# Window attention, a rational FFN and a gated FFN on one core: block 0's first part divided among three engines by rule, weight words put together in PSUM, later attention tied to phases

## The chip, the core and the metric

The kernel runs on one core of one Trainium2 chip. The metric is the device time of one execution, in microseconds (us). Engines: TensorE (PE; its weight loads are PEld), VectorE (DVE), ScalarE (ACT), GpSimd (POOL), and SyncE (SP), which issues the DMAs.

## What is computed

Three layers follow one another. Attention has 4 x 8 heads of 64 features over 576 positions with a causal window of 64. Then 2304 tokens of 512 features go through an FFN with a rational function, 512 -> 2048 -> 512, and through a gated one, 512 -> 1536 -> 512.

```python
scores = scale * np.matmul(q, k.transpose(0, 1, 3, 2))
mask = (rel >= 0) & (rel < window)
scores = np.where(mask, scores, -1000000000.0)
attn = softmax(scores)
x = np.matmul(attn, v)

h = x @ w_in
P = a[0] + a[1] * h + a[2] * h**2 + a[3] * h**3
Q = 1.0 + np.abs(b[0]) * np.abs(h) + np.abs(b[1]) * h**2
x = (P / (Q + 1e-06)) @ w_out

gate = 1.0 / (1.0 + np.exp(-(x @ w_gate)))
return gate * (x @ w_val) @ w_out2
```

The weights arrive as 64-bit floats and the other inputs as 32-bit ones.

## The kernel before

**Precision.** Each fp32 product of the FFNs is three TensorE passes: an operand is split into a high part (rounded to the fp32r type, `hi`) and a low part (what is left, `lo`), and hi x hi, hi x lo and lo x hi are added in PSUM.

**Tiling.** The 2304 tokens are five blocks of 512, 256, 512, 512 and 512. The work of one block and one FFN is a phase: "part 1" is the rational FFN (`step1`, 16 steps f of 128 hidden features), "part 2" the gated one (`step2`, 12 steps). Phases run: part 1 and 2 of block 0, then part 1 of blocks 1 and 2, part 2 of blocks 1 and 2, and so for 3 and 4. A step of part 1 is 12 matmuls into a PSUM bank h, a chain of elementwise operations, and 12 matmuls into four y banks. A step of part 2 has 12 matmuls each into h (gate) and a (value), a sigmoid, a product, the split, and 12 matmuls into y.

**The chain of a step of part 1** (line of the kernel before in brackets): `size` |h| (730) and `cubic` a3 h (734) on ScalarE; `slope` (739, 743) and `quad` (748), which make Q; two `horner` steps (751) on VectorE, with h from PSUM; `log` (757) and `seed` exp (760) on ScalarE, a first 1/Q; `check` (763) and `newton` (768) refine it, or `check`, `rest` (774, 776) and `correct` (779) do the same in three; `ratio` (782); `hi` (316 ScalarE, 318 VectorE, 320 GpSimd) and `lo` (323).

**Attention.** A unit is 128 tokens and all heads: units 0 to 3 belong to block 0, 4 and 5 to block 1, 6 to 9 to block 2, and so on. In each: scores (546, 557), peak (571), exps (579), inverse (588, 589), norm (593), transposes on TensorE (604) or, from unit 10, on VectorE (621), values (630), and the split into x.

**Weights.** A chunk is 128 x 512. In the first use of each chunk its 64-bit floats are turned into fp32 with integer instructions: DMA into `wraw` (3 tiles), `rescale` (414, 416) of the high word into a temporary `wt`, `sign` (422 VectorE, 427 GpSimd), `shift` (430) and `low_bits` (435) on VectorE, then `hi` and `lo`. Chunks that are used again are stored to DRAM and loaded from there (477). In block 0's first part 32 such chunks (w_in and w_out) are made, in its second part 36.

**What sets the order.** The kernel doesn't write its order by hand. Each operation is registered with a due time (`prio`), the engines that may do it with a cost each (`ways`), what it needs (`deps`), and the tile slots that it takes and uses. `Plan.order` places the operations one after the other: at each moment, by due time, each goes to the engine that would end it first by these costs, if its slots are free; `PORT` marks costs that GpSimd and VectorE may not spend at the same time. The result is one list; each engine works through its part in that order at run time, and waits where an input isn't there. Slots: 28 chunks w, 3 wraw (s), 11 temporaries t, 2 split tiles g; PSUM has 8 banks: 4 y, 2 h, 2 a.

Of the kernel before, what the change touches and what calls it, by code (L numbers as in the profile page):

```python
# [216 lines left out]
def pe(n, count=1):  # L217
    return ("PE", count * (n / 2400 + 0.0025))


def act(n, psum=False, ptrs=0):
    return ("ACT", n / 1200 + (0.05 if psum else 0.093) + 0.093 * ptrs)


def dve(n, ptrs=0):

    return ("DVE", n / 960 + 0.15 + 0.03 * ptrs, *PORT)
# [7 lines left out]
def dve2(n, ptrs=0):  # L235
    return ("DVE", n / 1920 + 0.15 + 0.03 * ptrs, *PORT)
# [6 lines left out]
def pool1(n, ptrs=0):  # L243
    return ("POOL", n / 960 + 0.07 + 0.03 * ptrs, *PORT)
# [7 lines left out]
def tile_window_attention__rational_ffn__glu(  # L252
# [58 lines left out]
    def temp(slot, name, dt=F32):  # L311
        return tile_of(slot, [P, 512], dt, name)
# [83 lines left out]
    def weights(c, prio, keys, again):  # L396

        raw_s, t_s, w_s = Slot("s"), Slot("t"), Slot("w")  # L400
        z = {}
# [6 lines left out]
        def rescale(e):  # L408
            t = z["t"] = temp(t_s, "wt", U32)
            w = z["c"] = tile_of(w_s, [P, 2, 512], F32R, "w")  # L410
            z["hi"], z["lo"] = w[:, 0, :], w[:, 1, :]
            x = z["high"].bitcast(F32)
            if e == "ACT":
                nc.scalar.activation(out=t.bitcast(F32), in_=x, func=AF.Copy, scale=REBIAS * REBIAS)  # L414
            else:
                ENGINES[e].tensor_scalar(
                    out=t.bitcast(F32), in0=x, scalar1=REBIAS, scalar2=REBIAS, op0=ALU.mult, op1=ALU.mult
                )
# [27 lines left out]
        def store(e):  # L446
# [4 lines left out]
        o = before["load"] = op(  # L451
            -200.47 + 0.92 * before.get("n", 0) if before.get("n", 0) < 8 else prio - 6.66,
            [dma(4096 * P)], load, takes=[raw_s], after=before.get("load")
        )
        before["n"] = before.get("n", 0) + 1
        o = before["size"] = before["take"] = op(
            prio, [act(512), dve2(512), pool1(512)], rescale, [o, before.get("size")], [t_s, w_s], [raw_s],
            before.get("take"),
        )
        o = op(prio, [pool1(512), dve2(512)], sign, [o], uses=[raw_s])  # L460
        o = op(prio, [dve(512)], shift, [o], uses=[t_s, raw_s])
        o = op(prio, [dve(512)], low_bits, [o], uses=[t_s, raw_s])
# [25 lines left out]

    def unit(u, t0, prio_load, prio_v):
        first_block = u < UB[0]  # L490
# [175 lines left out]
        for j in range(2):  # L666
            o = sc = op(
                t(j), [pe(512, (5 if first_block else 4) + on_pe)], scores(j), [lk, sc],
                [s_s[j]] + [sm_s][j:], {q_s, k_s},
# [44 lines left out]
    def step1(p, b, fs, f, t0):  # L714
# [97 lines left out]
        G = op(t0 + 1.06, [act(n, True, 1)], cubic, [H, coef], [g_s], [h_s])  # L812
        Q = op(t0 + 2.74, [dve2(n, 2), act(n, False, 2), pool1(n, 2)], slope, [A, coef], [q_s], [a_s])
        Q = op(t0 + 1.97, [pool(n), dve(n)], quad, [Q], uses=[q_s, a_s])
        G = op(t0 + 0.94, [dvep(n, 1)], horner(2), [G], uses=[g_s, h_s])
# [3 lines left out]
        Q = op(t0 + 0.6, [dve(n)], check, [L], uses=[r_s, q_s])  # L819
        if b == 0 and f % 4 < 1:  # L820
            Q = op(t0 + 0.6, [act(n, False, 1), dve2(n), pool1(n)], rest, [Q], uses=[q_s])
            L = op(t0 + 2.52, [pool(n), dve(n)], correct, [Q], uses=[r_s, q_s])
        else:
            L = op(t0 + 2.52, [dve(n)], newton, [Q], uses=[r_s, q_s])
        G = op(t0 + 4.38, [dve(n, 1)], ratio, [L, G], uses=[r_s, g_s])
        X = op(t0 + 4.16, [act(n), dve2(n), pool1(n)], hi, [G], [gs_s], [g_s])
        X = op(t0 + 3.61, [pool(n), dve(n)], lo, [X], uses=[gs_s, g_s])
        for ms in [range(KD)] if f != last_f else [(m,) for m in range(KD)]:
# [30 lines left out]
    def step2(p, b, fs, f, t0):  # L859
# [221 lines left out]
```

## Time and profile before

| | us |
|---|---|
| median of 3 runs | 1024.69 |
| lowest, highest | 1024.28, 1024.74 |
| profiled execution | 1018.68 |
| its span, first to last instruction | 1016.9 |
| PE busy | 960.3 (94%) |
| DVE busy | 725.7 (71%) |
| ACT busy | 484.8 (48%) |
| POOL busy | 200.7 (20%) |

The page divides the span into 40 slices of 25.4 us and gives each engine's busy share in tenths. A "group" is all instructions of one line, engine and operation: busy time, the mean of one, and the idle time just before them with what ended it. An instruction's shown duration overlaps the next one's start by some tens of nanoseconds, so what one costs in a full queue is the distance between two starts; the busy time of a window counts overlapped time once.

### The profile page before, as it was taken

How to read it: one execution, taken by the hardware profiler on the slowest of the kernel's cores; microseconds unless marked ns; L12 is line 12 of the kernel's file. 1: busy time of each engine (PE TensorE's matmuls, PEld its weight loads, DVE VectorE, ACT ScalarE, POOL GpSimd, SP SyncE). 2: the span in 40 equal slices, each digit the busy share in tenths (PEclk: the TensorE clock that was granted, in tenths of full speed). 3: DMA queues.
4: the chain of work that ended last, by engine and by line, in shares of the span. 5: the costliest groups of instructions: out<-in, count | busy, mean ns of one | idle time of the engine just before them, and what ended most of it. 6: DMA issues, size and time to landing. Idle time of an engine off the chain costs nothing.

```text
span 1016.9 us, 14241 instructions
## 1 busy us (share of the span) xinstructions
PE 960.3 (94%) x5120; PEld 798.7 (79%) x5120; DVE 725.7 (71%) x1272; ACT 484.8 (48%) x974; POOL 200.7 (20%) x215
## 2 busy tenths in 40 slices
PE   8977777689999998999999999999999999999998
PEld 6855555468888996888998888888888888888886
DVE  5999899988888899886887765688998932222222
ACT  3775667445567874655443432565666610001001
POOL 3331232121313452231000110223232200000000
PEclk7998978699999998999999999999999999999999
DMA  9645655979999523556526675410155541005001
GB/s 291 233 145 210 245 206 197 336 257 313 318 313 345 184 68 107 197 193 223 161 63 218 211 221 179 145 63 1 47 181 188 193 158 63 1 21 186 1 1 41
DMA packets 72677, 170.92 MB, mean 168 GB/s; under 512 B 20704, under 2 KB 29920, under 8 KB 72608
## 3 DMA queue, kind: packets, MB, share of 16 engines
q1 hardware_dynamic: 72608, 170.03, 50.0%
q8 instruction: 40, 0.66, 0.3%
q14 instruction: 29, 0.24, 0.1%
HBM read 129.63 MB, written 40.37 MB: 167 GB/s over the span
## 4 chain that ended last, share of the span: by engine, by line
PE 78%; DVE 11%; DMA 6%; ACT 3%; issue 2%; POOL 0%; SPq 0%; DVEq 0%; ACTq 0%; POOLq 0%
PE h L705 29%; PE y L705 28%; PE a L705 14%; DMA wraw<-in_moe_w_out_dram 2%; DMA wraw<-in_moe_w_in_dram 2%; PE a L557 2%; DVE tg L751 2%; DVE wt L435 2%; PE a L630 1%; DVE tq L763 1%; DVE wt L430 1%; PE y L557 1%; DVE w L323 1%; PE a L380 1%; DMA qk<-in_k_dram 1%
## 5 line engine op out<-in xcount | busy, mean ns | idle before, releaser
L705 PE MATMUL h<-x,w 128*128 128x512 f32 (+1 forms) x1680 | 380.1, 376 | 15.0 <-ACT w L316 9.1
L705 PEld LDWEIGHTS h<-x,w 128*128 128x128 f32 x1680 | 299.9, 193 | 75.4 <-ACT w L316 11.7
L705 PE MATMUL y<-g,w 128*128 128x512 f32 (+1 forms) x960 | 225.9, 386 | 19.8 <-DVE g L323 11.8
L705 PEld LDWEIGHTS y<-g,w 128*128 128x128 f32 x960 | 176.0, 198 | 58.2 <-DVE g L323 14.6
L705 PE MATMUL a<-x,w 128*128 128x512 f32 (+1 forms) x720 | 160.2, 372 | 4.7 <-ACT sm L579 3.5
L705 PE MATMUL y<-w,g 128*128 128x512 f32 x648 | 158.6, 392 | 0.3 <-DVE w L323 0.3
L882 ACT ACTIVATE sg<-h 128x512 f32<-128x512 f32 (+1 forms) x60 | 33.3, 555 | 246.1 <-PE h L705 246.0
L705 PEld LDWEIGHTS a<-x,w 128*128 128x128 f32 x720 | 127.1, 190 | 28.8 <-ACT sm L579 3.9
L705 PEld LDWEIGHTS y<-w,g 128*128 128x128 f32 x648 | 120.0, 188 | 24.8 <-DVE w L323 0.6
L751 DVE SCALAR_TENSOR_TENSOR tg<-tg,ca_sb,h 128x512 f32<-128x512 f32 (+1 forms) x160 | 108.1, 688 | 24.4 <-ACT ta L730 16.6
L885 DVE TENSOR_TENSOR sg<-sg,a 128x512 f32<-128x512 f32 (+1 forms) x60 | 37.8, 633 | 121.7 <-PE a L705 118.8
L748 POOL TENSOR_TENSOR tq<-tq,ta 128x512 f32<-128x512 f32 (+1 forms) x62 | 80.4, 1299 | 123.0 <-ACT tq L739 121.5
L757 ACT ACTIVATE tr<-tq,biases 128x512 f32<-128x512 f32 (+1 forms) x80 | 54.3, 678 | 56.7 <-POOL tq L748 53.8
L734 ACT ACTIVATE tg<-h,ca_sb 128x512 f32<-128x512 f32 (+1 forms) x80 | 51.6, 645 | 52.9 <-PE h L705 52.6
L763 DVE SCALAR_TENSOR_TENSOR tq<-tq,tr 128x512 f32<-128x512 f32 (+1 forms) x80 | 54.2, 679 | 17.3 <-ACT tr L760 16.5
L427 POOL TENSOR_SCALAR wraw<-wraw 128x512 f32<-128x512 f32 x38 | 32.3, 849 | 163.4 <-ACT wt L414 151.5
L414 ACT ACTIVATE wt<-wraw 128x512 f32<-128x512 f32 x59 | 39.8, 674 | 49.0 <-DMA wraw<-in_moe_w_out_dram 24.5
L782 DVE SCALAR_TENSOR_TENSOR tg<-tg,ca_sb,tr 128x512 f32<-128x512 f32 (+1 forms) x80 | 61.9, 774 | 0.6
L768 DVE SCALAR_TENSOR_TENSOR tr<-tq,tr 128x512 f32<-128x512 f32 (+1 forms) x76 | 57.5, 760 | 0.2
L621 DVE STREAM_TRANSPOSE et<-sm 32x256 f32<-32x256 f32 x128 | 55.8, 436 | 2.3
L318 DVE CAST g<-sg 128x512 fp32r<-128x512 f32 (+1 forms) x42 | 17.1, 408 | 56.0 <-PE y L705 55.5
L760 ACT ACTIVATE tr<-tr,biases 128x512 f32<-128x512 f32 (+1 forms) x80 | 54.4, 680 | 1.8
(94 smaller groups left out, 957.0 us busy)
## 6 DMA issues: line engine op xcount, KB each, us to landing
w<-wo SPq DMA_DIRECT2D x32, 512.0 KB, 3.3
w<-wp SPq DMA_DIRECT2D x32, 512.0 KB, 3.3
wraw<-in_moe_w_out_dram SPq DMA_DIRECT2D x28, 512.0 KB, 4.7
w<-wg SPq DMA_DIRECT2D x28, 512.0 KB, 3.3
w<-wv SPq DMA_DIRECT2D x28, 512.0 KB, 3.3
w<-wi SPq DMA_DIRECT2D x20, 512.0 KB, 3.3
vv<-in_v_dram SPq DMA_DIRECT2D x35, 256.0 KB, 3.9
wraw<-in_moe_w_in_dram SPq DMA_DIRECT2D x16, 512.0 KB, 4.4
```

The costliest lines, as they stand in the source:

```text
L414: nc.scalar.activation(out=t.bitcast(F32), in_=x, func=AF.Copy, scale=REBIAS * REBIAS)
L621: nc.vector.transpose(out=to[cols, :, rows], in_=at[rows, :, cols])
L705: nc.tensor.matmul(p, lhs(a), rhs(b), start=first and n == 0, stop=last and n == 2)
L734: nc.scalar.activation(out=z["g"], in_=z["h"], func=AF.Copy, scale=ca_sb[:, 3:4])
L748: ENGINES[e].tensor_tensor(out=z["q"], in0=z["q"], in1=z["a"], op=ALU.mult)
L751: return lambda e: nc.vector.scalar_tensor_tensor(out=z["g"], in0=z["g"], scalar=ca_sb[:, m:m + 1], in1=z["h"], op0=ALU.add, op1=ALU.mult)
L757: nc.scalar.activation(out=z["r"], in_=z["q"], func=AF.Ln, scale=LN_SCALE, bias=lnb)
L760: nc.scalar.activation(out=z["r"], in_=z["r"], func=AF.Exp, scale=-1.0, bias=exb)
L763: nc.vector.scalar_tensor_tensor(out=z["q"], in0=z["q"], scalar=1.0 + 1e-6, in1=z["r"], op0=ALU.add, op1=ALU.mult)
L768: nc.vector.scalar_tensor_tensor(out=z["r"], in0=z["q"], scalar=2.0, in1=z["r"], op0=ALU.subtract, op1=ALU.mult, reverse0=True)
L782: nc.vector.scalar_tensor_tensor(out=z["g"], in0=z["g"], scalar=ca_sb[:, 0:1], in1=z["r"], op0=ALU.add, op1=ALU.mult)
L885: nc.vector.tensor_tensor(out=z["t"], in0=z["t"], in1=z["v"], op=ALU.mult)
```

## The change

Four things. (1) In block 0's first part the chain has fixed engines: `slope`, `rest` and `hi` ScalarE; `quad`, `correct` and `lo` GpSimd; both `horner`, `check` and `ratio` VectorE. `rest` and `correct` now serve all 16 steps, `newton` none of block 0. (2) From the ninth chunk on, those of w_in and w_out (24) put their word together in a PSUM bank (`wb`, from the 2 a banks) instead of a temporary in SBUF; `rescale` and `hi` are then ScalarE's, `sign` GpSimd's, `shift`, `low_bits` and `lo` VectorE's. (3) The scores of later blocks' units are registered phase by phase and wait for a hidden product three steps before the end of the phase before theirs. (4) The planner counts 11 ns more for a matmul of over 256 columns, and the `hi` of the steps follow one another in a fixed order.

```diff
 def pe(n, count=1):
-    return ("PE", count * (n / 2400 + 0.0025))
+    return ("PE", count * (n / 2400 + (0.0135 if n > 256 else 0.0025)))
...
-        raw_s, t_s, w_s = Slot("s"), Slot("t"), Slot("w")
+        n = before.get("n", 0)
+        before["n"] = n + 1
+        banked = c[0] in "io" and n >= 8
+        raw_s, t_s, w_s = Slot("s"), Slot("a" if banked else "t"), Slot("w")
...
-            t = z["t"] = temp(t_s, "wt", U32)
+            t = z["t"] = tile_of(t_s, [P, 512], U32, "wb" if banked else "wt")
...
+        one, two = (dvep(512), [act(512, True)]) if banked else (dve(512), [act(512), dve2(512), pool1(512)])
         o = before["size"] = before["take"] = op(
-            prio, [act(512), dve2(512), pool1(512)], rescale, [o, before.get("size")], [t_s, w_s], [raw_s],
+            prio, two, rescale, [o, before.get("size")], [t_s, w_s], [raw_s],
             before.get("take"),
         )
-        o = op(prio, [pool1(512), dve2(512)], sign, [o], uses=[raw_s])
-        o = op(prio, [dve(512)], shift, [o], uses=[t_s, raw_s])
-        o = op(prio, [dve(512)], low_bits, [o], uses=[t_s, raw_s])
-        o = op(prio, [act(512), dve2(512), pool1(512)], hi, [o], uses=[t_s, w_s])
-        o = op(prio, [pool(512), dve(512)], lo, [o], uses=[t_s, w_s])
+        o = op(prio, [pool1(512)] if banked else [pool1(512), dve2(512)], sign, [o], uses=[raw_s])
+        o = op(prio, [one], shift, [o], uses=[t_s, raw_s])
+        o = op(prio, [one], low_bits, [o], uses=[t_s, raw_s])
+        o = op(prio, two, hi, [o], uses=[t_s, w_s])
+        o = op(prio, [one] if banked else [pool(512), dve(512)], lo, [o], uses=[t_s, w_s])
...
-    def unit(u, t0, prio_load, prio_v):
+    def unit(u, t0, prio_load, prio_v, gate=None):
...
-                t(j), [pe(512, (5 if first_block else 4) + on_pe)], scores(j), [lk, sc],
+                t(j), [pe(512, (5 if first_block else 4) + on_pe)], scores(j), [lk, sc, gate],
...
-        Q = op(t0 + 2.74, [dve2(n, 2), act(n, False, 2), pool1(n, 2)], slope, [A, coef], [q_s], [a_s])
-        Q = op(t0 + 1.97, [pool(n), dve(n)], quad, [Q], uses=[q_s, a_s])
+        Q = op(t0 + 2.74, [dve2(n, 2), act(n, False, 2), pool1(n, 2)] if b else [act(n, False, 2)], slope, [A, coef], [q_s], [a_s])
+        Q = op(t0 + 1.97, [pool(n), dve(n)] if b else [pool(n)], quad, [Q], uses=[q_s, a_s])
...
-        if b == 0 and f % 4 < 1:
-            Q = op(t0 + 0.6, [act(n, False, 1), dve2(n), pool1(n)], rest, [Q], uses=[q_s])
-            L = op(t0 + 2.52, [pool(n), dve(n)], correct, [Q], uses=[r_s, q_s])
+        if b == 0:
+            Q = op(t0 + 0.6, [act(n, False, 1)], rest, [Q], uses=[q_s])
+            L = op(t0 + 2.52, [pool(n)], correct, [Q], uses=[r_s, q_s])
         else:
             L = op(t0 + 2.52, [dve(n)], newton, [Q], uses=[r_s, q_s])
...
-        X = op(t0 + 4.16, [act(n), dve2(n), pool1(n)], hi, [G], [gs_s], [g_s])
-        X = op(t0 + 3.61, [pool(n), dve(n)], lo, [X], uses=[gs_s, g_s])
+        X = prev_h["g"] = op(t0 + 4.16, [act(n), dve2(n), pool1(n)] if b else [act(n)], hi, [G], [gs_s], [g_s], prev_h.get("g"))
+        X = op(t0 + 3.61, [pool(n), dve(n)] if b else [pool(n)], lo, [X], uses=[gs_s, g_s])
...
-    for b, (start, end) in spans.items():
-        for o in range(UB[b]):
-            t0 = start + o * (end - start) / UB[b] - 4.41
-            unit(U0[b] + o, t0, t0 - 1, t0)
...
     for p, (part, b, fs, t0) in enumerate(phases):
+        for x, (start, end) in spans.items():
+            if t0 <= start < t0 + (part + 1) * len(fs):
+                for o in range(UB[x]):
+                    t1 = start + o * (end - start) / UB[x] - 4.41
+                    unit(U0[x] + o, t1, t1 - 1, t1, gates.get(p))
         for i, f in enumerate(fs):
+            if i == len(fs) - 3:
+                gates[p + 1] = prev_h["h"]
```

**VectorE in the middle of block 0's first part, before.** The names: tg, tq, tr are the chain's tiles, ta is |h|, h a PSUM bank, wt a chunk's word in SBUF, wraw its 64-bit floats, w and g the split chunk and the split product.

```order
L751 SCALAR_TENSOR_TENSOR tg<-tg,ca_sb,h 128x512 x4
L430 SCALAR_TENSOR_TENSOR wt<-wt,wraw 128x512 x2
L763 SCALAR_TENSOR_TENSOR tq<-tq,tr 128x512
L435 SCALAR_TENSOR_TENSOR wt<-wraw,wt 128x512 x2
L782 SCALAR_TENSOR_TENSOR tg<-tg,ca_sb,tr 128x512
L323 TENSOR_TENSOR w<-wt,w 128x512 x2
L323 TENSOR_TENSOR g<-tg,g 128x512
L779 TENSOR_TENSOR tr<-tq,tr 128x512
L430 SCALAR_TENSOR_TENSOR wt<-wt,wraw 128x512
L748 TENSOR_TENSOR tq<-tq,ta 128x512
L435 SCALAR_TENSOR_TENSOR wt<-wraw,wt 128x512
L422 TENSOR_SCALAR wraw<-wraw 128x512
```

**The same engine and place, changed kernel** (its lines are 4 higher after the first hundreds; wb is a chunk's word in a PSUM bank).

```order
L767 SCALAR_TENSOR_TENSOR tq<-tq,tr 128x512
L434 SCALAR_TENSOR_TENSOR wb<-wb,wraw 128x512 x2
L439 SCALAR_TENSOR_TENSOR wb<-wraw,wb 128x512 x2
L755 SCALAR_TENSOR_TENSOR tg<-tg,ca_sb,h 128x512
L323 TENSOR_TENSOR w<-wb,w 128x512 x2
L786 SCALAR_TENSOR_TENSOR tg<-tg,ca_sb,tr 128x512
```

The low part of g, correct or newton, quad and sign are no longer in VectorE's queue; the three instructions of each chunk stay, with wb in the place of wt.

**ScalarE in the same stretch, before.** L316 writes a high part (of a chunk w or of g), L414 is a rescale.

```order
L414 ACTIVATE wt<-wraw 128x512 x2
L734 ACTIVATE tg<-h,ca_sb 128x512
L757 ACTIVATE tr<-tq,biases 128x512
L730 ACTIVATE ta<-h 128x512
L760 ACTIVATE tr<-tr,biases 128x512
L739 ACTIVATE tq<-ta,cb_sb 128x512
L414 ACTIVATE wt<-wraw 128x512
L316 CAST w<-wt 128x512
L316 CAST g<-tg 128x512
```

**ScalarE, changed kernel.**

```order
L418 ACTIVATE wb<-wraw 128x512
L761 ACTIVATE tr<-tq,biases 128x512
L316 CAST w<-wb 128x512
L764 ACTIVATE tr<-tr,biases 128x512
L418 ACTIVATE wb<-wraw 128x512
L738 ACTIVATE tg<-h,ca_sb 128x512
L734 ACTIVATE ta<-h 128x512
L778 ACTIVATE tq<-tq,biases 128x512
L743 ACTIVATE tq<-ta,cb_sb 128x512
L316 CAST w<-wb 128x512 x2
```

A rescale (L418) now stands one instruction behind the cast of the chunk that held the bank before it, and `rest` (L778) is in every step.

**TensorE at the start of block 0's first part, before.** kt and q_diag are k and q of unit 4.

```order
L705 MATMUL h<-x,w 128x512 x24
L546 LDWEIGHTS ident_100
L546 MATMUL a<-maskn,ident_100 128x512
L557 MATMUL a<-kt,q_diag 128x128 x4
L546 LDWEIGHTS ident_100
L546 MATMUL a<-maskf,ident_100 128x512
L557 MATMUL a<-kt,q_diag 128x128 x4
L705 MATMUL h<-x,w 128x512 x36
```

**TensorE, changed kernel, from the twelfth hidden product.**

```order
L709 MATMUL h<-x,w 128x512 x24
L709 MATMUL y<-g,w 128x512 x12
L550 LDWEIGHTS ident_100
L550 MATMUL a<-maskn,ident_100 128x512
L561 MATMUL a<-kt,q_diag 128x128 x4
L709 MATMUL h<-x,w 128x512 x12
L709 MATMUL y<-g,w 128x512 x12
```

Unit 4's scores moved from behind the second hidden product to behind the thirteenth; the 60 first matmuls of the phase now follow one another.

## Rows read from the trace of the kernel before

**Rows 1.** The page's busy tenths of TensorE and VectorE in 40 equal slices of the span.

```profile
PE   8977777689999998999999999999999999999998
...
DVE  5999899988888899886887765688998932222222
```

**Rows 2.** Busy time by stretch. Columns: the stretch (us from the span's start), its length, then busy us (and instructions) of each engine, TensorE's granted clock as a share of 2.4 GHz, DMA share, GB/s.

```profile
40.50:204.10 163.60, 123.76 (x479) 92.68 (x479) 151.11 (x242) 107.10 (x198) 39.94 (x38) 0.84 0.65 232
...
204.10:216.40 12.30, 8.79 (x60) 6.65 (x59) 10.12 (x19) 8.42 (x17) 3.47 (x5) 0.86 0.87 297
216.40:312.80 96.40, 94.89 (x498) 78.05 (x497) 84.20 (x147) 53.38 (x105) 19.44 (x23) 1.00 0.90 304
312.80:371.20 58.40, 57.98 (x493) 55.61 (x492) 48.70 (x109) 44.70 (x125) 27.77 (x38) 1.00 0.59 196
371.20:399.40 28.20, 24.05 (x139) 19.83 (x139) 27.45 (x51) 15.54 (x29) 11.61 (x13) 0.89 0.29 94
399.40:1016.90 617.50, 613.70 (x3077) 514.92 (x3075) 375.21 (x639) 235.19 (x424) 85.07 (x77) 1.00 0.38 124
```

**Rows 3.** The chain that ended last, from 400 to 410 us: start, length, what.

```profile
405.33 2.72 PE h L705 x12
```

**Rows 4.** What TensorE waited for from 40 to 205 us: its line, the engine and line waited for, us in total, times, longest.

```profile
PE y L705 <- DVE g L323: 9.9, 6, 2.2
PE h L705 <- ACT w L316: 9.1, 5, 2.9
```

**Rows 5.** Timeline of VectorE: start, us, engine, line, operation, tiles, shapes, count.

```profile
46.42 0.74 DVE L751 SCALAR_TENSOR_TENSOR tg<-tg,ca_sb,h 128x512 f32<-128x512 f32 x1
...
61.52 0.68 DVE L430 SCALAR_TENSOR_TENSOR wt<-wt,wraw 128x512 uint32<-128x512 uint32 x1
62.12 0.68 DVE L323 TENSOR_TENSOR g<-tg,g 128x512 fp32r<-128x512 f32 x1
...
70.01 1.77 DVE L323 TENSOR_TENSOR w<-wt,w 128x512 fp32r<-128x512 f32 x1
...
82.82 0.42 DVE L422 TENSOR_SCALAR wraw<-wraw 128x512 uint32<-128x512 uint32 x1
83.16 0.41 DVE L318 CAST w<-wt 128x512 fp32r<-128x512 f32 x1
```

**Rows 6.** Timeline of GpSimd, same columns.

```profile
45.98 1.67 POOL L748 TENSOR_TENSOR tq<-tq,ta 128x512 f32<-128x512 f32 x1
...
69.52 1.72 POOL L748 TENSOR_TENSOR tq<-tq,ta 128x512 f32<-128x512 f32 x1
```

**Rows 7.** VectorE's groups from 40 to 205 us, shapes kept apart: count, busy us, mean ns of one, idle before.

```profile
L323 DVE TENSOR_TENSOR w<-wt,w 128x512 fp32r<-128x512 f32 x32 | 26.9, 858 | 2.1 <-ACT w L316 2.1
L435 DVE SCALAR_TENSOR_TENSOR wt<-wraw,wt 128x512 uint32<-128x512 uint32 x34 | 22.6, 681 | 0.0
L751 DVE SCALAR_TENSOR_TENSOR tg<-tg,ca_sb,h 128x512 f32<-128x512 f32 x32 | 22.0, 735 | 0.0
...
L323 DVE TENSOR_TENSOR g<-tg,g 128x512 fp32r<-128x512 f32 x15 | 12.3, 822 | 0.0
...
L763 DVE SCALAR_TENSOR_TENSOR tq<-tq,tr 128x512 f32<-128x512 f32 x16 | 12.0, 750 | 7.3 <-ACT tr L760 7.2
L768 DVE SCALAR_TENSOR_TENSOR tr<-tq,tr 128x512 f32<-128x512 f32 x12 | 10.0, 833 | 0.0
...
L323 DVE TENSOR_TENSOR x<-a,x 128x512 fp32r<-128x512 f32 x2 | 1.3, 669 | 0.0
```

**Rows 8.** GpSimd's groups from 40 to 205 us, same columns.

```profile
L427 POOL TENSOR_SCALAR wraw<-wraw 128x512 f32<-128x512 f32 x22 | 18.5, 839 | 109.3 <-ACT wt L414 107.5 <-DVE wt L430 1.8
...
L323 POOL TENSOR_TENSOR g<-tg,g 128x512 fp32r<-128x512 f32 x1 | 1.3, 1295 | 0.0
```

**Rows 9.** ScalarE's groups from 40 to 205 us, same columns.

```profile
L739 ACT ACTIVATE tq<-ta,cb_sb 128x512 f32<-128x512 f32 x14 | 11.4, 814 | 2.5 <-POOL tq L748 2.3
...
L774 ACT ACTIVATE tq<-tq,biases 128x512 f32<-128x512 f32 x3 | 2.2, 722 | 6.2 <-DVE tq L763 6.2
```

**Rows 10.** Timeline of TensorE at the turn to block 2: start, us, what, count, and in brackets the idle time before with its releaser.

```profile
389.26 1.52 PE L630 MATMUL a<-et,vv 128*64 128x64 f32 x30 [2.08 <-DVE et L621]
390.71 2.08 PE L557 MATMUL a<-kt,q_diag 128*128 128x128 f32 x8
...
395.48 4.10 PE L705 MATMUL y<-g,w 128*128 128x512 f32 x11 [1.91 <-DVE g L323]
```

**Rows 11.** Timelines of ScalarE, VectorE and TensorE, same columns: two chunks from rescale to low part (the second is the first of the pair at 98.44), and transposes of attention with their copy.

```profile
80.92 0.70 ACT L414 ACTIVATE wt<-wraw 128x512 f32<-128x512 f32 x1 [1.58 <-DMA wraw<-in_moe_w_out_dram]
83.94 0.68 ACT L414 ACTIVATE wt<-wraw 128x512 f32<-128x512 f32 x1 [2.32 <-DMA wraw<-in_moe_w_in_dram]
...
89.42 1.12 DVE L323 TENSOR_TENSOR w<-wt,w 128x512 fp32r<-128x512 f32 x1
98.44 1.28 DVE L323 TENSOR_TENSOR w<-wt,w 128x512 fp32r<-128x512 f32 x2
...
197.06 1.11 PE L604 MATMUL a<-ident,sm 128*128 128x128 f32 x4 [4.25 <-POOL sm L593]
...
198.78 0.59 ACT L316 COPY et<-a 128x512 f32<-128x512 f32 x1
```

**Rows 12.** Timeline of TensorE where block 0's second part begins, same columns.

```profile
204.11 0.93 PE L705 MATMUL h<-x,w 128*128 128x512 f32 x3
```

More of the change, by code (lines that the diff above doesn't have):

```diff
@@ L451, in weights @@
         o = before["load"] = op(
-            -200.47 + 0.92 * before.get("n", 0) if before.get("n", 0) < 8 else prio - 6.66,
+            -200.47 + 0.92 * n if n < 8 else prio - 6.66,
             [dma(4096 * P)], load, takes=[raw_s], after=before.get("load")
         )
-        before["n"] = before.get("n", 0) + 1
+        one, two = (dvep(512), [act(512, True)]) if banked else (dve(512), [act(512), dve2(512), pool1(512)])
         o = before["size"] = before["take"] = op(
-            prio, [act(512), dve2(512), pool1(512)], rescale, [o, before.get("size")], [t_s, w_s], [raw_s],
+            prio, two, rescale, [o, before.get("size")], [t_s, w_s], [raw_s],
             before.get("take"),
         )
-        o = op(prio, [pool1(512), dve2(512)], sign, [o], uses=[raw_s])
-        o = op(prio, [dve(512)], shift, [o], uses=[t_s, raw_s])
-        o = op(prio, [dve(512)], low_bits, [o], uses=[t_s, raw_s])
-        o = op(prio, [act(512), dve2(512), pool1(512)], hi, [o], uses=[t_s, w_s])
-        o = op(prio, [pool(512), dve(512)], lo, [o], uses=[t_s, w_s])
+        o = op(prio, [pool1(512)] if banked else [pool1(512), dve2(512)], sign, [o], uses=[raw_s])
[3 more added lines that the diff above has]
+        o = op(prio, [one] if banked else [pool(512), dve(512)], lo, [o], uses=[t_s, w_s])
         for key in keys:
@@ L836, in tile_window_attention__rational_ffn__glu @@
     prev_h = {}
+    gates = {}
     first = []
@@ L915, in step2 @@
         o = op(t0 + 2.2, [dvep(n)], gated, [o, mm["v"]], uses=[t_s, p_s["v"]])
-        o = op(t0 + 2.4, [act(n), dve2(n), pool1(n)], hi, [o], [gs_s], [t_s])
+        o = prev_h["g"] = op(t0 + 2.4, [act(n), dve2(n), pool1(n)], hi, [o], [gs_s], [t_s], prev_h.get("g"))
         o = op(t0 + 2.6, [pool(n), dve(n)], lo, [o], uses=[t_s, gs_s])
```

## The prediction

> **What bounds the kernel now.** I read the page's slices first [rows 1]: TensorE is at 9 tenths in all but the first third, and there it stands at 7 while VectorE is at 8 to 9. The busy times by stretch [rows 2] give the place a name. From 40.5 to 204.1 us, block 0's first part, VectorE is busy 151.1 of 163.6 us (92%), ScalarE 107.1, GpSimd 39.9. TensorE shows 123.8, but its need is less: a group of 12 matmuls takes 2.72 us at full clock [rows 3], and 16 steps of two groups are 87 us. From 216.4 on TensorE is close to full: 94.9 of 96.4, 58.0 of 58.4, 24.1 of 28.2, 613.7 of 617.5. What TensorE waits for in the first stretch [rows 4] are products of VectorE and ScalarE, in small pieces. So the first part is VectorE's, the rest TensorE's, with one hole at 386 to 399 us.
>
> **The change, part by part.** *VectorE's list.* Counted in the order from the first cubic's horner step to the first gated product. Off VectorE go 15 low parts of g, 12 newton, 6 quad, 4 correct, 2 norm, 2 low parts of w, a shift and a low_bits: 43 two-tensor instructions; and 11 sign, 4 casts and 1 rest, less one rescale that comes: 15 of one tensor; and two tiny ones (0.2). Starts of back-to-back ones lie 0.60 and 0.34 us apart (61.52 and 62.12; 82.82 and 83.16 [rows 5]): 43 x 0.60 + 15 x 0.34 + 0.2 = 31.1 us off.
>
> *The shared access.* GpSimd and VectorE hold each other up where VectorE reads two tensors of SBUF: at 70.01 a low part takes 1.77 instead of 0.68 us, beside a GpSimd quad from 69.52 that takes 1.72 [rows 5, 6]. With h in PSUM it doesn't happen: at 46.42 it took 0.74 beside GpSimd's quad from 45.98 [rows 5, 6], and the 32 of the stretch take 0.735 in the mean [rows 7]. Over the stretch the SBUF forms lie above the 0.681 of L435 by 0.177 x 32 (low parts of w), 0.141 x 15 (of g), 0.152 x 12 (newton) and 0.069 x 16 (check): 10.7 us [rows 7], for the 39.9 us in which GpSimd is busy. A low part or product costs GpSimd 1.295 alone, a sign 0.84 [rows 8]. It gets 16 correct, 14 low parts and 6 quads at 1.30 and some 11 signs at 0.84: 56 us more, 96 in all. Exposed on VectorE stay 60 two-tensor SBUF instructions instead of 171 (check, ratio, and the chunks that still use SBUF). At 0.27 us per us of GpSimd work and 60/171 x 164/137 of the density, that is 96 x 0.27 x 0.42 = 10.9 us: as much as before. Below: nothing. Above: 1.09 us for each of the 60, 65 us.
>
> *Weight bits in PSUM.* 24 chunks build their word in a bank; 72 VectorE instructions read or write PSUM. No row shows VectorE writing PSUM. Reading it costs the same: 0.669 for a low part from PSUM against 0.681 for L435 in SBUF [rows 7]. I take 0.60 apart as now; bounds 0.55 to 0.70, 4 us less or 7 more. [...]
>
> So VectorE's work in the stretch is 151.1 - 31.1 - 11 + 11 = 120 us.
>
> *ScalarE* gets 13 rest (0.722 less the 0.10 by which neighbours overlap) and 2 slopes (0.814 less the same) [rows 9]; 4 more casts of w stand against 4 rescales less: 13 x 0.62 + 2 x 0.71 = 9.5 us, 117 in all. That was far off the path and is now beside it.
>
> *How long the stretch gets.* At no wait at all, 120 us; at VectorE's present 92%, 130. I take 137 (88%), nearer to that row than to the 163.6 of no gain, because ScalarE is then at 85% instead of 65%, and because a wait is added: a rescale into a bank stands in ScalarE's queue until VectorE's low part has freed it, and log, seed and rest stand behind it, for which check and ratio wait on VectorE, and low parts on GpSimd. DMA doesn't forbid it: 232 GB/s x 163.6 us are 38 MB, and 304 GB/s were moved from 216 to 313 [rows 2], so 125 us suffice. Saved: 163.6 - 137 = 26.6.
>
> *The fixed order of the high parts* on one engine's tile, the costs in the planner (a matmul of 512 at 0.227, what [rows 3] show) and the scores tied to step 13 cost nothing of their own: the scores of unit 4 leave the 46 us place, and both units still run before the second part, as before. Their cover is the tail of y groups; without it unit 4's two score blocks are 2 us.
>
> *The hole at 386 to 399.* There unit 10's values wait 2.08 us for VectorE's transposes, then y 1.91, and at the low clock level 11 matmuls take 4.10 instead of 2.49 and 8 scores 2.08 instead of 1.05 [rows 10]: 6.6 us. Counted in the order, unit 10's scores and the 8 of unit 11 move some 85 us of matmuls later, behind step 13 of block 2's first part. Late next is what its VectorE work meets in its new place, where VectorE is busy 375 of 617 us [rows 2]; and the y groups of the turn stay. I take 4.5 us saved, bounds 0 and 6.6.
>
> Sum: 1016.9 - 26.6 - 4.5 = 985.8 span, 987.6 with the 1.8 around it; the profiled run (1018.68) lies 6.0 under the median of the runs (1024.69), so 994.
>
> **Rivals.** *The two banks set the pace (slower).* ScalarE's order shows each rescale into a bank just behind the cast of the one before it in that bank. With L from a rescale to the next one in that bank, 24 chunks take 12 L; some 5 us pass before the first, and the 11 bank uses of attention in the tail take 16 more (about 3 us each over two banks, an estimate from the transposes at 197.06 to the end of their copy at 199.37 [rows 11]). The stretch is then 21 + 12 L. Before, with plenty of tiles, a chunk took 9.6 us (80.92 to 90.54) and 15.2 (83.94 to 99.1) [rows 11], counted in their order. 9.6 gives 136, my value; above 11.9 nothing is gained, and at 13.2 the stretch takes 179, 16 us more: with the 4.5 saved 1036. For it: all hops through four queues in fixed order, and GpSimd twice as busy. Against: those 9.6 to 15.2 were spent behind VectorE's backlog of 92%, and that shrinks.
>
> *The shared access takes the gain.* If each of the 60 waits 0.6 us, half of what 70.01 lost, that is 36 instead of 11 us: VectorE 145, at 92% 157, saved 6.6 + 4.5: 1014. At 1.09 each it would be slower than before. [...] Against it: only two of VectorE's ten instructions in a step read two SBUF tensors now, and the rows of h beside GpSimd show no loss.
>
> *The gain is not in the stretch.* The second part starts earlier but its g, v and p chunks don't come earlier, at a DMA share of 0.90 [rows 2]; TensorE would wait there. 20 us given back: 1014. Against: these 36 chunks need no more VectorE than before, and the same number is ready at the turn.
>
> **How the numbers follow.** My forecast 0.72, with 977 to 1009 (stretch 120 to 152); banks 0.12; access 0.10; given back 0.06. The range of 977 to 1019 leaves out most of the banks' case and a little below. Within 0.2% (some 2 us, about what a measurement of this kernel can tell) is a narrow strip between the cases, 0.04; faster 0.72 + 0.10 + 0.04 = 0.86; slower, all from the banks, 0.10.
>
> **What would show it.** The first matmul of the second part (204.11 now [rows 12]) near 177, block 0's still near 40.5; in between VectorE near 120 and ScalarE near 117 us busy, GpSimd near 96; the new low parts with PSUM near 0.68 us whatever GpSimd does; no wait of values at the turn to block 2; TensorE full after that. I am wrong if ScalarE's rescale waits for VectorE's low part come to over 20 us, if check and ratio take over 1.1 us in the mean, or if TensorE stands still in the second part.

## The result and the profile after

The changed kernel takes 990.37 us in the median of four runs (987.78 to 993.58), against 1024.72 us for the kernel before (1024.28 to 1026.61): a ratio of 0.9687, with a 95% interval of 0.9645 to 0.973. 994 us were forecast. The profiled execution took 987.78 us, its span 986.0, where 985.8 were worked out. That these two agree within 0.2 us is in part luck: the profile of the kernel before lies 6.0 us under its median and this one 2.6 under its own, so that 30.9 us of the gain are seen in the traces and 34.4 in the medians.

The page's slices of the changed kernel, as [rows 1], with GpSimd's and the clock's:

```profile
PE   8978877899999999999999999999999999999998
...
DVE  5879998888898899897877763888897632222221
...
POOL 4377675211234444430011100300122100000000
PEclk7999998999999999999999999999999999999999
```

From the third slice to the eighth TensorE stands at 7 to 8 where it stood at 6 to 7, and GpSimd has 2 to 7 tenths there. By stretch, with the columns of [rows 2], come block 0's first part, up to the first matmul of the second, and then the stretches that answer to those of before.

```profile
39.94:184.12 144.18, 113.07 (x512) 85.61 (x511) 126.81 (x189) 114.25 (x214) 93.26 (x86) 0.93 0.74 258
184.12:197.90 13.78, 13.78 (x65) 11.41 (x62) 12.19 (x24) 10.68 (x20) 4.29 (x5) 1.00 0.81 308
...
342.00:369.60 27.60, 26.96 (x149) 23.22 (x149) 25.61 (x46) 16.78 (x31) 13.25 (x14) 1.00 0.35 115
369.60:986.00 616.40, 612.38 (x3109) 513.70 (x3107) 378.01 (x644) 247.52 (x456) 78.76 (x75) 1.00 0.39 124
```

The first matmul of the second part stands at 184.12 instead of 204.11 [rows 12]. That is a bad mark, though: in the 12.3 us that follow it before, TensorE was busy for 8.79 and its granted clock was 0.86 in the mean [rows 2]; now it is busy throughout there, at 1.00. VectorE's first gated product (`sg<-sg,a`) is a better one, since the same matmuls lie ahead of it and behind it: at 216.54 before, 189.97 after. First the two windows of before, then those of after:

```profile
40.46:216.54 176.08, 132.73 (x537) 99.51 (x536) 161.27 (x260) 115.66 (x214) 43.41 (x42) 0.84 0.66 237
216.54:1016.90 800.36, 790.47 (x4201) 668.27 (x4199) 535.55 (x943) 348.67 (x681) 143.88 (x149) 1.00 0.46 149
```

```profile
39.94:189.97 150.03, 118.92 (x538) 90.45 (x537) 132.39 (x200) 118.59 (x222) 95.00 (x89) 0.93 0.74 259
189.97:986.00 796.03, 787.73 (x4201) 665.56 (x4199) 534.63 (x936) 361.41 (x706) 138.37 (x145) 1.00 0.46 153
```

So 26.1 us went in the first window, 4.3 in the rest (4201 matmuls in both kernels) and 0.5 ahead of the start: 30.9, the difference of the spans. A second profile of the changed kernel (`bank8_again`, below) tells how well such windows repeat: the first window is 3.0 us longer, the rest the same.

```profile
38.96:191.98 153.02, 122.44 (x538) 93.44 (x537) 132.56 (x200) 118.64 (x222) 95.40 (x89) 0.90 0.73 255
191.98:988.00 796.02, 787.70 (x4201) 665.62 (x4199) 533.51 (x936) 361.34 (x705) 135.52 (x145) 1.00 0.46 153
```

In the first window VectorE has 28.9 us less to do, and is busy for 88% of it (before 92%); GpSimd has 51.6 us more.

VectorE's groups from 40 to 187 us, which answer to [rows 7]:

```profile
L434 DVE SCALAR_TENSOR_TENSOR wb<-wb,wraw 128x512 uint32<-128x512 uint32 x24 | 16.4, 695 | 2.1 <-POOL wraw L431 2.1
L439 DVE SCALAR_TENSOR_TENSOR wb<-wraw,wb 128x512 uint32<-128x512 uint32 x24 | 16.3, 689 | 0.2
L323 DVE TENSOR_TENSOR w<-wb,w 128x512 fp32r<-128x512 f32 x24 | 16.1, 683 | 1.7 <-ACT w L316 1.6
L767 DVE SCALAR_TENSOR_TENSOR tq<-tq,tr 128x512 f32<-128x512 f32 x16 | 14.1, 881 | 3.4 <-ACT tr L764 3.4
L786 DVE SCALAR_TENSOR_TENSOR tg<-tg,ca_sb,tr 128x512 f32<-128x512 f32 x16 | 13.9, 867 | 0.0
L439 DVE SCALAR_TENSOR_TENSOR wt<-wraw,wt 128x512 uint32<-128x512 uint32 x9 | 8.3, 921 | 0.0
L323 DVE TENSOR_TENSOR w<-wt,w 128x512 fp32r<-128x512 f32 x9 | 8.1, 897 | 1.2 <-ACT w L316 1.1
L434 DVE SCALAR_TENSOR_TENSOR wt<-wt,wraw 128x512 uint32<-128x512 uint32 x10 | 7.8, 789 | 0.0
```

Three of a chunk's instructions, on the word in PSUM (`wb`), take 0.68 to 0.70 us. The same three on a word in SBUF (`wt`) take 0.79 to 0.92, and the two instructions of a step that read two SBUF tensors 0.87 and 0.88. GpSimd's groups over the same time [rows 8], and ScalarE's `rescale` into a bank with its `hi`:

```profile
L752 POOL TENSOR_TENSOR tq<-tq,ta 128x512 f32<-128x512 f32 x16 | 23.0, 1435 | 6.4 <-ACT tq L743 6.3
L323 POOL TENSOR_TENSOR g<-tg,g 128x512 fp32r<-128x512 f32 x16 | 21.1, 1321 | 15.0 <-ACT g L316 15.0
L783 POOL TENSOR_TENSOR tr<-tq,tr 128x512 f32<-128x512 f32 x16 | 21.1, 1320 | 6.6 <-ACT tq L778 6.6
```

```profile
L418 ACT ACTIVATE wb<-wraw 128x512 f32<-128x512 f32 x24 | 15.2, 637 | 0.8 <-DMA wraw<-in_moe_w_out_dram 0.6
L316 ACT CAST w<-wb 128x512 fp32r<-128x512 f32 x24 | 13.8, 581 | 2.5 <-DVE wb L439 2.4
```

ScalarE stood 0.8 us in all ahead of the 24 rescales into banks, mostly for a DMA.

### The profile page after: what moved, and what is told of

Its sections match the earlier page's. It is cut to its first block, busy times and chain, and to the rows that moved or that the text cites. A ratio compares the mean times of both kernels' runs of the same rounds, so it can differ in the third digit from the quotient of the medians.

```text
span 986.0 us, 14185 instructions
## 1 busy us (share of the span) xinstructions
PE 943.6 (96%) x5110; PEld 786.5 (80%) x5110; DVE 694.5 (70%) x1203; ACT 502.0 (51%) x1010; POOL 247.7 (25%) x258
## 4 chain that ended last, share of the span: by engine, by line
PE 78%; DVE 5%; ACT 3%; issue 2%; POOL 1%; DMA 1%; SPq 0%; POOLq 0%; ACTq 0%; DVEq 0%
PE y L709 31%; PE h L709 29%; PE a L709 14%; PE a L561 2%; PE a L634 2%; DVE tg L755 1%; DVE w L323 1%; ACT tg L738 1%; DVE tq L767 1%; DVE wb L434 0%; ACT sm L583 0%; POOL wraw L431 0%; DMA wraw<-in_moe_w_gate_dram 0%; DVE tg L786 0%; DMA q_diag<-in_q_dram 0%
## 5 line engine op out<-in xcount | busy, mean ns | idle before, releaser
L709 PE MATMUL h<-x,w 128*128 128x512 f32 (+1 forms) x1680 | 372.0, 371 | 9.4 <-ACT w L316 4.2
L709 PEld LDWEIGHTS h<-x,w 128*128 128x128 f32 x1680 | 294.2, 189 | 67.0 <-ACT w L316 5.6
L709 PE MATMUL y<-g,w 128*128 128x512 f32 (+1 forms) x960 | 220.6, 379 | 12.4 <-POOL g L323 4.5
L709 PEld LDWEIGHTS y<-g,w 128*128 128x128 f32 x960 | 171.6, 194 | 49.6 <-POOL g L323 6.0
L752 POOL TENSOR_TENSOR tq<-tq,ta 128x512 f32<-128x512 f32 (+1 forms) x59 | 77.2, 1308 | 59.6 <-ACT tq L743 46.9
L767 DVE SCALAR_TENSOR_TENSOR tq<-tq,tr 128x512 f32<-128x512 f32 (+1 forms) x80 | 57.3, 716 | 15.5 <-ACT tr L764 15.1
L747 POOL TENSOR_SCALAR tq<-ta,cb_sb 128x512 f32<-128x512 f32 (+1 forms) x26 | 21.6, 831 | 146.7 <-ACT ta L734 144.1
L318 DVE CAST g<-sg 128x512 fp32r<-128x512 f32 (+1 forms) x37 | 15.1, 409 | 56.7 <-PE y L709 56.3
L431 POOL TENSOR_SCALAR wraw<-wraw 128x512 f32<-128x512 f32 x48 | 36.2, 757 | 72.7 <-ACT wt L418 34.2
L734 ACT ACTIVATE ta<-h 128x512 f32<-128x512 f32 (+1 forms) x80 | 43.8, 549 | 4.0 <-DVE tg L755 4.0
```

Source lines behind the costliest of these rows:

```text
L431: nc.gpsimd.tensor_scalar(out=x, in0=x, scalar1=0.0, scalar2=0.0, op0=ALU.mult, op1=ALU.mult)
L709: nc.tensor.matmul(p, lhs(a), rhs(b), start=first and n == 0, stop=last and n == 2)
L734: nc.scalar.activation(out=z["a"], in_=z["h"], func=AF.Abs)
L752: ENGINES[e].tensor_tensor(out=z["q"], in0=z["q"], in1=z["a"], op=ALU.mult)
L767: nc.vector.scalar_tensor_tensor(out=z["q"], in0=z["q"], scalar=1.0 + 1e-6, in1=z["r"], op0=ALU.add, op1=ALU.mult)
```

## The experiments

The theory that goes with the forecast (A in most of the expectations): the rule takes 31 us off VectorE's list, and that is the gain; the word in PSUM costs nothing and keeps the added GpSimd work from holding VectorE up. Its rivals: the banks are the gain, or nothing without the rule.

**Each half taken out of the change, and put into the kernel before.** Without the banks:

```diff
-        banked = c[0] in "io" and n >= 8
+        banked = False
```

> The changed kernel with every chunk's word in an SBUF temporary, on the engines that the planner picks, as before; all else of the change stays. Theory A (block 0's first part lasts as long as VectorE's work there, waits at the access that it shares with GpSimd included): VectorE has 135 two-tensor SBUF instructions in the stretch instead of 60, beside the same GpSimd work; 0.27 us x 96 us of GpSimd work x the higher density is some 13 us more waiting, and some 19 more one-tensor instructions of 0.34 are 6.5: about 20 us of stretch, 1008 to 1014. Theory B (the pace is set by the hops of a step's chain through three engines, which the fixed engines cut; where the word lies is no matter): 988 to 995.

Measured 1022.57 us, ratio 1.0026 (0.9991 to 1.0062). Both missed: not a part of the gain, all of it is gone. Without the rule for block 0's steps (the banks stay):

```diff
-        Q = op(t0 + 1.97, [pool(n), dve(n)] if b else [pool(n)], quad, [Q], uses=[q_s, a_s])
+        Q = op(t0 + 1.97, [pool(n), dve(n)], quad, [Q], uses=[q_s, a_s])
...
-        if b == 0:
-            Q = op(t0 + 0.6, [act(n, False, 1)], rest, [Q], uses=[q_s])
-            L = op(t0 + 2.52, [pool(n)], correct, [Q], uses=[r_s, q_s])
+        if b == 0 and f % 4 < 1:
+            Q = op(t0 + 0.6, [act(n, False, 1), dve2(n), pool1(n)], rest, [Q], uses=[q_s])
+            L = op(t0 + 2.52, [pool(n), dve(n)], correct, [Q], uses=[r_s, q_s])
```

and `slope`, `hi` and `lo` likewise.

> The changed kernel with the engines of block 0's chain left to the planner as before (newton in three steps of four); banks, phases and costs stay. Theory A: 28 more two-tensor instructions on VectorE (17 us) and some 5 of one tensor (2 us), less some port waits as GpSimd does less: 13 to 17 us more, 1002 to 1008. Theory B: nearly all of the gain goes, 1015 to 1025.

Measured 996.44 us, ratio 0.9774 (0.9738 to 0.981). That is 6 us more than the changed kernel by the medians and 9 by the ratios: less than A gave the rule and far less than its rival. The reverse of both, the kernel before with one part alone: the rule's lines,

```diff
-        Q = op(t0 + 1.97, [pool(n), dve(n)], quad, [Q], uses=[q_s, a_s])
+        Q = op(t0 + 1.97, [pool(n), dve(n)] if b else [pool(n)], quad, [Q], uses=[q_s, a_s])
```

(and the others of that function),

> The kernel before with only the fixed engines of block 0's chain. Theory A: VectorE loses the work that moves to GpSimd and ScalarE, but its 135 two-tensor SBUF instructions wait for a GpSimd that is twice as busy, and the hole at block 2 stays: 1012 to 1019. Theory B: most of the gain is here, 992 to 1000.

or the words in PSUM with their engines:

```diff
-        raw_s, t_s, w_s = Slot("s"), Slot("t"), Slot("w")
+        n = before.get("n", 0)
+        before["n"] = n + 1
+        banked = c[0] in "io" and n >= 8
+        raw_s, t_s, w_s = Slot("s"), Slot("a" if banked else "t"), Slot("w")
```

> The kernel before with only the words of the 24 chunks in PSUM banks and the engines that go with it. Theory A: about 16 two-tensor instructions and 10 of one tensor less on VectorE, 13 us, and some 6 us of waits at the shared access; the hole stays: 1003 to 1011. Theory B: no gain, 1020 to 1026.

The rule alone: 1029.26 us, ratio 1.0044 (1.0021 to 1.0067), a little slower than before. The banks alone: 994.26 us, ratio 0.9672 (0.9619 to 0.9725), which can't be told from the whole change. Both of A's ranges were missed, in opposite directions. The windows from block 0's first hidden product to the first gated product say why. They start at different times (34.7 to 43.7 us), and even a kernel and its twin with the same order of instructions can differ by 7 us there (44.26 and 36.81, the pair with nine temporaries below), so the end of a window is to be read beside its length. First the rule alone, then the banks alone, then (third fence) the changed kernel without banks:

```profile
34.74:227.61 192.87, 141.74 (x538) 101.31 (x537) 162.04 (x222) 126.53 (x231) 92.42 (x66) 0.81 0.58 206
```

```profile
43.72:203.41 159.69, 124.30 (x546) 91.91 (x545) 144.64 (x235) 108.54 (x212) 78.48 (x81) 0.91 0.78 267
```

```profile
42.68:230.68 188.00, 137.81 (x538) 99.12 (x537) 160.08 (x220) 124.26 (x227) 90.69 (x68) 0.85 0.58 208
```

With the rule alone VectorE has 222 instructions where it had 260, and is busy 162.0 us where it was busy 161.3: what was taken off its list came back as longer instructions. The banks alone took only 25 off, but there the busy time falls by 16.6 us, to 144.6: the planner, which counts no shared access for a word in PSUM, gave that work to GpSimd by itself (78.5 us busy, before 43.4), and little of it came back as longer instructions (its groups on two SBUF tensors take 0.68 to 0.78 us in the mean, but for a single quad of 1.78). With the rule alone, VectorE's groups in that window, and one of GpSimd's:

```profile
L430 DVE SCALAR_TENSOR_TENSOR wt<-wt,wraw 128x512 uint32<-128x512 uint32 x35 | 28.7, 839 | 0.1
L435 DVE SCALAR_TENSOR_TENSOR wt<-wraw,wt 128x512 uint32<-128x512 uint32 x36 | 28.7, 815 | 0.0
L323 DVE TENSOR_TENSOR w<-wt,w 128x512 fp32r<-128x512 f32 x33 | 25.8, 801 | 7.5 <-ACT w L316 7.5
...
L422 DVE TENSOR_SCALAR wraw<-wraw 128x512 uint32<-128x512 uint32 x23 | 20.3, 888 | 3.3 <-ACT wt L414 3.3
L782 DVE SCALAR_TENSOR_TENSOR tg<-tg,ca_sb,tr 128x512 f32<-128x512 f32 x16 | 17.1, 1066 | 0.0
...
L323 POOL TENSOR_TENSOR g<-tg,g 128x512 fp32r<-128x512 f32 x16 | 29.5, 1841 | 54.1 <-ACT g L316 54.0
```

In the timeline of the rule alone, VectorE and GpSimd around 110 us, how that happens:

```profile
108.26 1.65 DVE L430 SCALAR_TENSOR_TENSOR wt<-wt,wraw 128x512 uint32<-128x512 uint32 x1
109.83 1.49 DVE L422 TENSOR_SCALAR wraw<-wraw 128x512 uint32<-128x512 uint32 x1
111.25 1.78 DVE L435 SCALAR_TENSOR_TENSOR wt<-wraw,wt 128x512 uint32<-128x512 uint32 x1
...
107.42 1.94 POOL L323 TENSOR_TENSOR g<-tg,g 128x512 fp32r<-128x512 f32 x1 [5.31 <-ACT g L316]
109.32 1.73 POOL L779 TENSOR_TENSOR tr<-tq,tr 128x512 f32<-128x512 f32 x1
111.00 1.48 POOL L748 TENSOR_TENSOR tq<-tq,ta 128x512 f32<-128x512 f32 x1
```

The two engines work in turns: each VectorE instruction ends 0.3 to 0.55 us after the GpSimd instruction that began before it (109.91 after 109.36; 111.32 after 111.05; 113.03 after 112.48), so that 0.68 us of work takes 1.65 and 1.78, and 0.42 takes 1.49. In the changed kernel, at 105 us:

```profile
104.42 0.69 DVE L439 SCALAR_TENSOR_TENSOR wb<-wraw,wb 128x512 uint32<-128x512 uint32 x1
105.10 0.70 DVE L434 SCALAR_TENSOR_TENSOR wb<-wb,wraw 128x512 uint32<-128x512 uint32 x1
105.83 0.69 DVE L439 SCALAR_TENSOR_TENSOR wb<-wraw,wb 128x512 uint32<-128x512 uint32 x1
...
105.13 1.28 POOL L752 TENSOR_TENSOR tq<-tq,ta 128x512 f32<-128x512 f32 x1
```

Neither is held up. The rest of what the rule loses is idle time: VectorE stood 30.8 us of the 192.9 (14.8 of 176.1 before), waiting mostly for ScalarE, while GpSimd waited 54.0 us for ScalarE's `hi` and ScalarE itself was busy for 66%. The four queues, in fixed order, wait round the circle; which of them was late first I didn't isolate.

**Is it PSUM, or the freed temporaries?** A word in a bank also leaves one of the 11 SBUF temporaries to others. So the changed kernel with nine temporaries,

```diff
-    POOLS = {"w": 28, "s": 3, "x": 3, "g": 2, "t": 11, "qt": 1, "kt": 1, "vv": 1, "sm": 1, "et": 1}
+    POOLS = {"w": 28, "s": 3, "x": 3, "g": 2, "t": 9, "qt": 1, "kt": 1, "vv": 1, "sm": 1, "et": 1}
```

> The changed kernel with 9 temporaries instead of 11; it is the measure for the next run, which needs the room. Theory A: the words have left the temporaries, so 9 are nearly enough: 988 to 996. Rival: the temporaries limit how many steps are in flight, and it is over 5 us slower.

and that kernel, its instructions in the same order, with the words in two tiles of SBUF of their own (attention then shares its two banks with no word):

```diff
+    word = ctx.enter_context(tc.tile_pool(name="p_wb", bufs=2))
...
-            t = z["t"] = tile_of(t_s, [P, 512], U32, "wb" if banked else "wt")
+            t = z["t"] = word.tile([P, 512], U32, tag="wb", name="wb") if banked else tile_of(t_s, [P, 512], U32, "wt")
```

> The same, in the same order of instructions on every engine, but the 24 words lie in two SBUF tiles of their own instead of two PSUM banks. Theory A: 72 more VectorE instructions read two SBUF tensors (or one SBUF and the word) and wait for GpSimd, 0.2 us each in the mean: 10 to 18 us slower than with 9 temporaries and banks, and their groups rise from 0.69 to 0.85 us or more. Theory B: no slower than that.

Nine temporaries: 998.18 us (ratio 0.9729, 0.9697 to 0.9761), 8 us above the changed kernel, as the rival had it. No run of the one reaches the runs of the other (995.91 at the least, 993.58 at the most), and the first gated product stands at 201.74 instead of 189.97; by the ratios, whose intervals overlap, it is 3 to 4 us. The same order with words in SBUF: 1016.72 us (0.9928, 0.9895 to 0.9962), 18.5 us slower on the same chip, the upper end of what A expected and a little over. The three groups on the word, first in PSUM, then in SBUF:

```profile
L434 DVE SCALAR_TENSOR_TENSOR wb<-wb,wraw 128x512 uint32<-128x512 uint32 x24 | 16.6, 692 | 1.7 <-POOL wraw L431 1.7
L439 DVE SCALAR_TENSOR_TENSOR wb<-wraw,wb 128x512 uint32<-128x512 uint32 x24 | 16.5, 690 | 0.4
L323 DVE TENSOR_TENSOR w<-wb,w 128x512 fp32r<-128x512 f32 x24 | 16.3, 684 | 1.0 <-ACT w L316 0.8
```

```profile
L435 DVE SCALAR_TENSOR_TENSOR wb<-wb,wraw 128x512 uint32<-128x512 uint32 x24 | 30.1, 1252 | 0.7 <-POOL wraw L432 0.7
L440 DVE SCALAR_TENSOR_TENSOR wb<-wraw,wb 128x512 uint32<-128x512 uint32 x24 | 28.5, 1190 | 0.4
L324 DVE TENSOR_TENSOR w<-wb,w 128x512 fp32r<-128x512 f32 x24 | 21.3, 892 | 0.8 <-ACT w L317 0.7
```

30.5 us more in 72 instructions. GpSimd's 87 instructions of the window take 108.7 us instead of 94.9, ScalarE waits 18.4 us for VectorE's `low_bits` instead of 2.7, and ScalarE's own 48 on the words take 1.9 us more. Every engine has the same instructions in the same order, so this is the price of the place, by itself.

**How it grows with the number of words.** Half of them, and two more:

```diff
-        banked = c[0] in "io" and n >= 8
+        banked = c[0] in "io" and n >= 20
```

> The changed kernel with the word in PSUM for 12 of the 24 chunks only (those from the 21st chunk built on, that is the later half of block 0's first part); the rest as changed. A (each banked chunk takes the same weight off the jam of GpSimd and VectorE): half of the 32 us between none banked (1022.6) and all (990.4), 1003 to 1010. B (the jam needs only to be relieved at some point, for the queue to catch up): under 998. C (as long as one stretch is jammed the planner's fixed engines fall behind for good): over 1015. In A the SBUF forms on wt lie near 0.81 to 0.87 us before the 21st chunk and the wb forms at 0.68 to 0.70 after it.

```diff
-        banked = c[0] in "io" and n >= 8
+        banked = c[0] in "io" and n >= 6
```

> The changed kernel with the word in PSUM for 26 chunks instead of 24 (from the 7th on). A (the gain grows with each banked chunk, 32 us over 24, 1.3 us each): 986 to 989. Rival (the two banks or ScalarE's queue are at their limit, or the early chunks have no GpSimd work beside them): 989 to 993, or slower.

Twelve words, those of the later half: 1007.05 us, ratio 0.9816 (0.9768 to 0.9863), within A's range. By the times that is half of the way from none to all, by the ratios (1.0026 and 0.9687) six tenths of it. In its trace the words in SBUF take 0.82 to 0.86 us and those in PSUM 0.68 to 0.69. Twenty-six words: 986.88 us, ratio 0.9631 (0.9573 to 0.9689), again as A said. Because that may beat the changed kernel, both ran once more on one chip:

> The changed kernel once more, as the control for the 26 banked chunks on the same chip: 988 to 993, ratio to the kernel before 0.965 to 0.972.

> 26 banked chunks, on the same chip as the control of 24. If the gain goes on growing with each banked chunk: 2 to 4 us below the control. Rival (the 986.9 of the first run was the scatter of these runs): within 2 us of it.

989.78 us (ratio 0.9702, 0.9665 to 0.9739) for 24 words and 985.80 (0.9667, 0.9626 to 0.9709) for 26. The median is lower by 3.5 and 4.0 us in the two comparisons, but the intervals overlap in both: it is likely a little better, and not shown.

**The tie to phases and the planner's cost.** The scores of later blocks without their wait:

```diff
-                    unit(U0[x] + o, t1, t1 - 1, t1, gates.get(p))
+                    unit(U0[x] + o, t1, t1 - 1, t1)
```

> The changed kernel without the wait of later units' scores on a hidden product of the phase before. Unit 10's scores stand again where they stood before the change. Theory A: the hole at the turn to block 2 comes back, 3 to 7 us more, 993 to 998, and block 0's stretch stays as it is. Rival: the hole was a matter of the turn and not of unit 10, then 988 to 993.

and the old cost of a matmul:

```diff
-    return ("PE", count * (n / 2400 + (0.0135 if n > 256 else 0.0025)))
+    return ("PE", count * (n / 2400 + 0.0025))
```

> The changed kernel with the planner's old cost of a matmul. Theory A: VectorE's list in block 0's first part is the same but for a few, so 988 to 994. Rival: the true cost puts the order of the later phases right, then TensorE has waits in them and it is 3 to 8 us slower, 994 to 999.

989.91 us (ratio 0.971, 0.9658 to 0.9761) and 989.07 us (0.9702, 0.9654 to 0.9751): neither does anything that can be measured in the time, and A's 993 to 998 for the first was missed. Without the tie the two waits at the turn to block 2 don't come back. Its profile isn't clean, though: TensorE has other waits there, 7.5 us from 205 to 420 instead of 4.0, and what lies behind the first gated product takes 798.7 us instead of 796.0, with 16 matmuls fewer:

```profile
191.67:990.40 798.73, 786.73 (x4185) 662.98 (x4183) 529.73 (x925) 360.84 (x705) 135.31 (x146) 1.00 0.46 152
```

What TensorE waited for in the kernel with the banks alone, which has no tie either, from 205 to 420 us:

```profile
PE h L708 <- DVE tg L754: 1.0, 2, 0.6
PE a L607 <- POOL sm L596: 0.6, 1, 0.6
```

In that kernel unit 10's scores stand where they stood before, and the 2.08 and 1.91 us of [rows 10] are not there.

## Why the prediction was right, and where its reason was wrong

*What bounds the kernel.* Right. Over all profiled runs the time behind the first gated product is 790 to 796 us, but for the kernel before (800.4) and the one without the tie (798.7), while that product itself stands at 189 to 231. What differs between the kernels is for the most part settled before it.

*VectorE's list*: 31.1 us less predicted, 28.9 measured to the first gated product, to which the list had been counted. What was mis-sized is the stretch that it was set against, which ended 12.4 us earlier, at 204.1. Up to the second part's first matmul VectorE has 126.8 us to do, not 120, and that matmul stands at 184.12, not at 177: 19.4 us saved there instead of 26.6. The other 6.6 were saved just behind it. From there to the first gated product it was 12.4 us, with TensorE idle for part of them and at a granted clock of 0.86, and is 5.9, with TensorE full at 1.00.

*The shared access*: 10.9 us predicted. In the window to 189.97 the forms that still read two SBUF tensors lie above what they take alone (0.681; the ratio 0.742, as at 105.94 with the rule alone) by 0.200 x 16 (check), 0.125 x 16 (ratio), 0.196 x 11, 0.098 x 11 and 0.216 x 9 (words in SBUF): 10.4 us. Right in size, and check and ratio stay under 0.9 us in the mean: the rival that gave each of 60 waits 0.6 us is out for this kernel.

*The word in PSUM at the price of SBUF*: 0.695, 0.689 and 0.683 us against 0.681; over 72 instructions that is 0.6 us, within the bounds.

*The stretch at 88%*: 88% (126.8 of 144.2 to the second part, 132.4 of 150.0 to the first gated product). The 26.1 us saved to the latter are near the 26.6 predicted for the former, by the mix of the two marks told above. ScalarE 114.3 and GpSimd 93.3 us busy to 184.12 (117 and 96 predicted). *The banks as the pace*: refuted by the 0.8 us ahead of the 24 rescales, and 26 words are no slower than 24. *Given back in the second part*: TensorE's waits from 200 us on come to some 4 us.

*The hole*: 4.5 us predicted for all that follows, 4.3 measured. The reason is not borne out. It was put down to unit 10's new place behind the tie. With the banks alone unit 10 has its old place and the waits are gone; with the rule alone, where there is no tie, the rest takes 794.7 us for the same 4201 matmuls. The run without the tie leaves it open whether some of the 4.3 us hang on the tie (798.7 against 796.0). What made the hole in the kernel before no run shows.

*The step that failed* is the reason of the whole: that the gain is VectorE's list made shorter by the rule, with the words in PSUM as what keeps the added work of GpSimd from costing anything. The total was right with the parts wrong. Without the banks A expected to keep some 10 to 17 us, and nothing is left; with the rule alone it expected 6 to 13, and there is no gain; with the banks alone 14 to 22, and they give the whole change within its interval. The words in PSUM take 72 instructions out of the shared access (0.68 to 0.70 us each in the mean; on a word in SBUF 0.79 to 0.92 in the same trace), give back temporaries, and hand `sign` and `rescale` to other engines. With the rule in place the first was priced by itself (18.5 us, at nine temporaries), the second at 3 to 8 us for two temporaries, the third not; for the banks alone, where 25 instructions also leave VectorE, the split was not measured.

What the rule adds to the banks is not well known. The first gated product comes 13.4 us earlier than with the banks alone (11.4 in the second profile), the part behind it takes 5.8 us longer (with 9 matmuls more in it), and the medians differ by 4 us, the ratios by nothing. Against the kernel without the rule it is 6 us and 9. These two kernels without the rule differ only in the tie, the planner's cost and the order of the high parts, of which the first two did nothing by themselves, and yet their ratios lie 1% apart, their medians 2 us. Either that order matters here, or a ratio can be off by more than its interval between two sets of runs.

The terms added up because the sum was made for both parts at once, with 60 instead of 171 instructions in the shared access. The same rate of 0.27 us held up per us of GpSimd was too low where the words stay in SBUF. There, with the rule alone, the five groups of VectorE shown above that touch it (L430, L435, L323, L422, L782) lie over what they take alone (the sign 0.423, the mean of its 13 before) by 5.5, 4.8, 4.0, 10.7 and 5.2 us: 30 us for 92.4 of GpSimd. A third of it is in a one-tensor form that the prediction hadn't counted as touching the access at all, and 16 us more of idle time on VectorE come on top, which no rate per instruction contains.

## What to carry to other kernels

Before work is moved from VectorE to GpSimd, count what VectorE still does on two SBUF tensors, or on one in the form that takes 0.42 us here: 38 instructions fewer bought nothing while the words lay in SBUF. In this kernel a temporary in PSUM cost VectorE about what one in SBUF does (0.683 to 0.695 us in the mean against 0.681) and was not held up (0.67 to 0.70 us in all 72), so it can be worth a bank for that alone, and it frees an SBUF tile besides. When a forecast is a sum of parts, price each part alone as well: the total can be right while the reason is not.

## What the runs showed of the hardware

The hold-up is not one of two-tensor forms alone. The sign, one SBUF tensor in and out, takes 0.42 us alone and 1.49 at 109.83 in the rule's timeline, 0.888 in the mean of 23. The words in PSUM, beside GpSimd's work in the changed kernel, took 0.69 to 0.70 us (104.42 to 105.83), with GpSimd's quad there at 1.28. Why the sign is held up and they are not, no run shows.

It works both ways: GpSimd's low part of g took 1.32 us in the mean with the words in PSUM and 1.84 with the rule alone (the one before 1.295 [rows 8]), and its 87 instructions of the pair with one order took 94.9 and 108.7 us.

The two engines took turns with the rule alone: VectorE's instructions at 108.26, 109.83 and 111.25 took 1.65, 1.49 and 1.78 us in a row, each over twice its time alone (0.68, 0.42 and 0.68).
